# Three loads of an RWKV-6 and MLP kernel moved to other places in the sync queue, and one gate moved with them

## The chip, the cores and the metric

The kernel runs on one core of a Trainium2 chip. The metric is the device time of one execution in microseconds, as the median of several executions. The engines are named as the profile names them: PE multiplies matrices (PEld loads its weights), DVE and POOL do elementwise work, ACT does activations and copies, and SP here does nothing but issue DMA transfers.

## The reference

Two blocks run one after the other. The first is a recurrent attention with a per-channel decay, for 4 sequences of 768 tokens and 8 heads of 48 channels:

```python
for t in range(S):
    cur = np.einsum('bhd,bhe->bhde', u[None] * kt, vt)
    y[:, :, t] = np.einsum('bhd,bhde->bhe', rt, state + cur)
    state = wt[:, :, :, None] * state + np.einsum('bhd,bhe->bhde', kt, vt)
```

Its output, as 3072 tokens of 384 channels, goes through a two-layer network with 2048 hidden channels:

```python
h = x @ w_in
sp = np.maximum(h, 0.0) + np.log1p(np.exp(-np.abs(h)))
g = h * erf(sp)
return (g @ w_out).astype(np.float32)
```

## The kernel before

The work is cut into 12 steps. A step is 128 tokens of two of the four sequences, all heads. Step 0 is written out by `attend_first`, steps 1 to 4 by `attend`, the rest by `attend_late`. Inside a step the attention over 128 tokens is built in levels 1 to 6: at each level PE forms products of r and k (`level_products`, line 554), DVE multiplies r and k in place by products of decays (`scale`, line 330) and merges the new products into `own` (`take_level`, line 564, or two ACT copies, line 571, at level 6). POOL makes the products of decays (`tot_sb`, lines 352 and 404) out of the step's `w`. Then `own` is multiplied by `v` (line 586), the state is updated (line 660 on PE, lines 852 or 957 on DVE) and the output of the step is transposed into `xT`.

The network of step s runs beside the attention of step s+1. `hidden` makes its first product in eight pieces. Piece n multiplies `xT` with pair n of the weights `w_in` (line 1019, 12 matrix instructions in the trace), leaves the result in one of two PSUM buffers called `m`, and ACT copies it out to `h` (line 1028). With two buffers, piece n can start only when the copy of piece n-2 is done.

The weights arrive as 64-bit floats. They are loaded two rows of tiles at a time, called a pair here: eight pairs of `w_in` (0 to 7), then eight of `w_out` (8 to 15). `convert` turns a pair into 32-bit floats in five stages: **l**, the load of the pair as two transfers of 384 KB each into one of three `words` buffers (line 147, called from `load`); **b** and **r**, two ACT instructions on the loaded words (lines 257 and 265); **h**, a DVE shift (line 274); **o**, a POOL addition (line 287). **j** is h followed by o. The table `CONVERT` says which stages are sent at which level of a step. For step 1 (`CONVERT[1]`) each level from the second to the fifth sends "j" early, that is, right after `scale`, and "brl" at `place`, after `take_level`:

```python
(("j", "br"),) + (("j", "brl"),) * 4 + (("j", "l"), ("", ""), ("", ""), ("", "brl")),
```

So at level 2 of step 1 the early "j" belongs to pair 3 and the late "brl" means b and r of pair 4 and the load of pair 5; at level 3 the same for pairs 4, 5 and 6; at level 4 for pairs 5, 6 and 7. The b and r of a pair stand on ACT ahead of the copy (line 1028) of a piece: those of pair 5 ahead of the copy of piece 2, those of pair 6 ahead of that of piece 3.

Engines run their instructions in the order in which they are written (`manual_schedule`). All transfers spoken of here are issued by SP, one after the other, and an issue that waits holds back all issues behind it. A **gate** is a one-element copy by POOL (line 242 or 185) or ACT (line 240) into the buffer that a transfer will fill: the transfer then cannot be issued before the copy is done, and the copy waits for the value that it copies.

The order of the loads of interest in SP's queue before the change is: pair 2 (gate on `seen`, line 829), pair 3 (gate on `xT` by ACT, line 634), pair 4 (line 635), `v` of step 1 (line 186, behind the gate in `load_third`, line 185, which copies an element of the new state `S_next`), pair 5, the two halves of r and k of step 2 (line 924), `w` of step 2 (line 925), pair 6, pair 7, pair 8. The state's sum `S_next` is written by DVE at line 852, in `pending`, which `attend` calls at level 2 of step 1 (line 903), before the early "j" of that level (line 905).

`w` of step 2 is read first by POOL at line 404, `v` of step 1 by PE at line 586 of step 1, and r and k of step 2 by ACT at line 382.

Of the kernel before, what the change touches and what calls it, by code (L numbers as in the profile page):

```python
# [61 lines left out]
def kernel(  # L62
# [14 lines left out]
    nc = tc.nc  # L77
# [51 lines left out]
    turns = {"next": 0}  # L129
# [10 lines left out]
    loaded = {}  # L140
# [3 lines left out]
    def load_halves(dst, src):  # L144

        for i in range(2):
            nc.sync.dma_start(out=dst[:, i], in_=src[:, i])

    def load_w(s):
        ws[s] = ins.tile([P, JP, C], FP32, name="w")  # L150
        nc.sync.dma_start(out=ws[s][:], in_=rkw[s][:, 2])
# [25 lines left out]
        nc.scalar.copy(t[:, 0, 0, 0:1], behind)  # L177
        load_halves(t, rkw[1])

    def load_third(behind):  # L180

        t = ins.tile([P, 2, JP, C], FP32, name="in")
        vt = ins.tile([P, NH, D], FP32, name="v")
        loaded[2] = t, vt
        nc.gpsimd.tensor_copy(out=loaded[1][1][:, 0, 0:1], in_=behind)
        load_v(1)

    def load_v(s):

        vt = loaded[s][1]  # L190
        nc.sync.dma_start(out=vt[:], in_=v[s])
# [29 lines left out]
    def convert(weights):  # L221

        held = {}
        plain = weights[0][1].dtype == FP32
        signed = len(weights) // 2

        def load(i, behind=None, by_scalar=False):
            if i >= len(weights):  # L230
                return
            dst, src = weights[i]
            if plain:
                nc.sync.dma_start(out=dst, in_=src)
                return
            words = wide.tile([P, 2, DM, 2], I32, name="words", bufs=3)
            if behind is not None:
                to = words[:, 0, 0, 0:1].bitcast(FP32)
                if by_scalar:
                    nc.scalar.copy(to, behind)  # L240
                else:
                    nc.gpsimd.tensor_copy(out=to, in_=behind)
            load_halves(words[:].rearrange("p i n two -> p i (n two)"), src.bitcast(I32))
            held[i] = {"words": words}

        def scale_high(i, part=slice(0, 2)):


            if i not in held:
                return  # L250
            if i < 2:
                base = ps_m.tile([P, NP * C], FP32, name="m")[:, :DM]
            else:
                base = y[:].rearrange("p e q j t -> p e (q j t)")[:, :, :DM]
            high = held[i]["words"][:, part, :, 1].bitcast(FP32)
            if i < signed:
                nc.scalar.activation(base, high, AF.Prelu, scale=2.0**-112, alpha=-(2.0**32))
            else:
                nc.scalar.mul(out=base, in_=high, mul=2.0**-112)
            held[i].setdefault("bases", []).append((base.bitcast(I32), part))  # L260

        def scale_low(i):
            if i in held:
                rest = wide.tile([P, 2, DM], I32, name="rest", bufs=2)
                nc.scalar.mul(  # L265
                    out=rest[:], in_=held[i]["words"][:, :, :, 0].bitcast(U32), mul=2.0**-29
                )
                held[i]["rest"] = rest

        def shift(i):  # L270
            if i in held:
                base, part = held[i]["bases"].pop(0)
                into = weights[i][0].bitcast(I32)[:, part]
                nc.vector.tensor_scalar(
                    out=into if i < signed else base, in0=base, scalar1=3, scalar2=None,
                    op0=ALU.logical_shift_left,
                )
                if i >= signed:
                    nc.vector.scalar_tensor_tensor(
                        out=into, in0=held[i]["words"][:, part, :, 1], scalar=-(1 << 31),  # L280
                        in1=base, op0=ALU.bitwise_and, op1=ALU.bitwise_or,
                    )

        def add(i):
            if i in held:
                into = weights[i][0].bitcast(I32)
                nc.gpsimd.tensor_tensor(
                    out=into, in0=into, in1=held.pop(i)["rest"][:], op=ALU.add
                )

        def join(i):
            shift(i)
            add(i)

        stages = {"l": load, "b": scale_high, "r": scale_low, "h": shift, "o": add, "j": join}
        done = {"l": 5, "b": 2, "r": 2, "j": 2}

        def send(what):
            for stage in what:
                stages[stage](done[stage])  # L300
                done[stage] += 1

        return stages, send

    def rows(e, n=D):
        return slice(e * EP, e * EP + n)

    def at(e, p):

        return rows(e ^ p & 1)  # L310
# [215 lines left out]
    def parts_of(s):  # L526

        c, i = divmod(s, SPC)
        in_t, vt = loaded[s]
        made, tots, tot = ready[s]  # L530
        ends = tot.rearrange("p (n h) -> p n h", h=NC)
        return c, in_t, vt, made, states[i][c % 2], states[i][1 - c % 2], ends
# [5 lines left out]
    def first_pair(x, n):  # L538

        return turns["first"][:, n // NP, x, n % NP]  # L540
# [59 lines left out]
    def through_state(s, xT):  # L600

        c, in_t, _, _, S, _, _ = parts_of(s)
        for h, state in enumerate((S, middle)):
            if not (c or h):
                continue
            t = slice(h * HC, (h + 1) * HC)
            for j, q in ((0, 2), (1, 2), (1, 0), (0, 0)) if not s else np.ndindex(NJ, NP // 2):
                q = q if not s else 2 * q
                for e in range(NE):
                    for p in (q + e, q + 1 - e):  # L610
                        n = j * NP + p
                        nc.tensor.matmul(  # L612
                            y[at(e, p), e, p // 2, j, t],
                            lhsT=state[rows(e), n, :],
                            rhs=(in_t[:, 0, n] if s else first_pair(0, n))[rows(e), t],
                            start=False, stop=True, skip_group_check=True,
                        )

        y3 = att.tile([P, UNIT], FP32, name="y3", bufs=1)
        nc.scalar.copy(y3[:].rearrange("p (j t) -> p j t", j=NJ), y[:, 1, 1])  # L620
        parts = y[:, 0, 0], y[:, 0, 1], y[:, 1, 0]
        by_kk = [xT[:, kk, :].rearrange("p (j t) -> p j t", j=NJ) for kk in range(KT)]
        if not s:

            def hop():
                for kk in range(KT):
                    nc.tensor.matmul(
                        parts[kk], lhsT=apart[:, kk],
                        rhs=y3[:].rearrange("p (j t) -> p j t", j=NJ),
                        start=False, stop=True, skip_group_check=True,  # L630
                    )
                for kk in range(KT):
                    nc.scalar.copy(by_kk[kk], parts[kk])
                stages["l"](3, xT[:, KT - 1, 0:1], True)
                stages["l"](4)

            turns["hop"] = hop
            return
        for kk in range(KT):
            nc.scalar.copy(by_kk[kk], parts[kk])  # L640
        by_scalar = {(kk, 1) for kk in range(KT) if s <= DIRECT}
        for kk in range(KT):
            n = D // KT
            for e in range(NE):
                queue = nc.scalar if (kk, e) in by_scalar else nc.sync
                queue.dma_start(
                    out=xT[e * EP + D : (e + 1) * EP, kk, :],
                    in_=y3[e * EP + kk * n : e * EP + (kk + 1) * n, :],
                )
# [97 lines left out]
    def attend_first(xT):  # L747
# [5 lines left out]
        c, _, vt, made, S, S_next, ends = parts_of(0)  # L753
# [25 lines left out]
        behind = {3: (3,), 4: (4, 5), 5: (6,)}  # L779
# [47 lines left out]
        stages["b"](1, 1)  # L827
        fence()
        stages["l"](2, seen[:, 0:1])
        stages["h"](0)  # L830
        stages["h"](0)
        ps = [[products([P, NE, JP, HC], 1 - e)[:, e] for e in range(NE)]]
# [15 lines left out]
        def pending():  # L848
            part = products([P, NE, JP, HC], turns["next"])[:, 0]
            state_part(0, kT, ps + [[part] * NE], (1,))  # L850
            for e in range(NE):
                nc.vector.tensor_add(S_next[rows(e)], faded[1][rows(e)], part[rows(e), :, :D])
            load_third(S_next[:, 0, 0:1])

        turns["pending"] = pending

# [18 lines left out]
    def attend(s, xT, early, place, behind):  # L875

        c, in_t, vt, made, S, S_next, ends = parts_of(s)
# [9 lines left out]
        for level in range(near_log(s) + 1 if s == DIRECT else 1, LOG + 1):  # L887
# [34 lines left out]
            place(level - 1)  # L922
            if s == 1 and level == 2:
                load_halves(loaded[2][0], rkw[2])
                load_w(2)

        from_own(s, own, 1)
        ps = products([P, JP, P])
# [526 lines left out]
```

## Time and profile before

| | |
|---|---|
| median of 3 runs | 593.79 us (592.19 to 594.02) |
| the profiled execution, its own time | 592.98 us |
| its span, first to last instruction | 591.2 us |
| PE busy in the span | 581.1 us (98%) |
| DVE, ACT, POOL busy | 437.8, 361.1, 270.8 us |
| mean granted clock of PE | 0.997 |
| DMA traffic | 63.24 MB, mean 107 GB/s |

The profile's times count from the start of the span. A timeline row gives start, duration, engine, line, operation, output and input, and in brackets the engine's idle time before it with what ended it. A row of the chain of waits gives start, duration and what ran. A row of the stretches gives, for each engine, its busy time and number of instructions, then PE's granted clock, the busy share of the DMA engines and the GB/s that they moved. In the timeline of PE, the rows whose bracket names more than half a microsecond of waiting are, after the first 2 us, just one: piece 5 of the hidden product of step 0, at 50.91 us.

### The profile page before, as it was taken

The numbers are of one execution on the slowest core, as the hardware profiler recorded it, in microseconds if no ns is written. First come the engines' busy times: TensorE is split into PE (matmuls) and PEld (weight loads), VectorE is DVE, ScalarE is ACT, GpSimd is POOL, SyncE is SP. The second block draws the span as 40 slices with busy tenths as digits, with TensorE's granted clock in tenths as the row PEclk, the third lists the DMA queues.
The fourth block names the chain that finished last, engine by engine and source line by source line (L and its number), as shares of the span: only waits on it lengthen the run. The fifth ranks groups of instructions, "written<-read, shape, count | busy, mean of one in ns | idle before, by whom it ended". The sixth has DMA issues, their size and how long they took to land.

```text
span 591.2 us, 16634 instructions
## 1 busy us (share of the span) xinstructions
PE 581.1 (98%) x7256; PEld 499.3 (84%) x7256; DVE 437.8 (74%) x523; ACT 361.1 (61%) x474; POOL 270.8 (46%) x308
## 2 busy tenths in 40 slices
PE   8997999999999999999999999999999999999997
PEld 6686887678668758998998898898898898898997
DVE  6794795899996899799799799799799525023140
ACT  4656878635544598756766766766766764746710
POOL 4546372701498569559359359359359000000000
PEclk9998999999999999999999999999999999999999
DMA  7587462541423414334334334333331300000000
GB/s 243 177 286 284 160 220 74 202 144 19 143 76 133 114 58 154 62 122 155 73 119 158 73 119 158 73 120 122 73 119 43 73 15 20 3 19 15 1 27 28
DMA packets 54082, 63.24 MB, mean 107 GB/s; under 512 B 35161, under 2 KB 40569, under 8 KB 52985
## 3 DMA queue, kind: packets, MB, share of 16 engines
q1 hardware_dynamic: 53624, 61.98, 33.0%
q8 instruction: 57, 0.93, 0.6%
q10 hardware_dynamic: 384, 0.20, 0.1%
q14 instruction: 17, 0.13, 0.1%
HBM read 52.39 MB, written 8.69 MB: 103 GB/s over the span
## 4 chain that ended last, share of the span: by engine, by line
PE 84%; DVE 9%; DMA 3%; ACT 2%; issue 2%; POOL 0%; SPq 0%; DVEq 0%; POOLq 0%; ACTq 0%
PE m L1019 37%; PE m L1127 28%; PE m L1051 6%; PE pp L554 4%; PE y L586 2%; DVE in L330 2%; DMA words<-in_moe_w_in 2%; PE pp L660 2%; PE y L612 2%; PE m L861 1%; DVE words L469 1%; DMA rest<-in_w_rows 1%; DVE rk L465 1%; DVE sums L455 1%; ACT rest L265 1%
## 5 line engine op out<-in xcount | busy, mean ns | idle before, releaser
L1019 PE MATMUL m<-xT,w_in_sb 128*128 128x256 f32 x1152 | 258.3, 383 | 3.1 <-ACT h L1028 3.0
L1019 PEld LDWEIGHTS m<-xT,w_in_sb 128*128 128x128 f32 x1152 | 217.3, 191 | 34.2 <-issue 3.3
L1028 ACT COPY h<-m 128x512 f32<-128x512 f32 x96 | 55.5, 579 | 83.2 <-PE m L1019 83.2
L330 DVE TENSOR_TENSOR in<-in,tot_sb 128x1024 f32<-128x1024 f32 (+1 forms) x55 | 78.2, 1423 | 16.2 <-PE pp L554 13.9
L465 POOL TENSOR_TENSOR rk<-words 128x528 f32<-128x528 f32 (+3 forms) x28 | 42.4, 1516 | 91.2 <-DVE sums L455 80.8
L469 POOL TENSOR_TENSOR words<-words,rest 128x528 f32<-128x528 f32 (+10 forms) x77 | 78.2, 1015 | 6.0
L1051 PE MATMUL m<-w_out_sb,h 128*128 128x384 f32 x192 | 64.3, 491 | 0.0
L1051 PEld LDWEIGHTS m<-w_out_sb,h 128*128 128x128 f32 x192 | 35.7, 190 | 23.5
L1127 PE MATMUL m<-mixed,h 128*128 128x192 f32 x288 | 51.1, 331 | 0.0
L975 ACT ACT_TABLE_LOAD x36 | 46.2, 1283 | 2.9 <-issue 2.3
L1127 PE MATMUL m<-w_out_sb,h 128*128 128x192 f32 x272 | 47.5, 329 | 0.0
L1127 PEld LDWEIGHTS m<-mixed,h 128*128 128x128 f32 x288 | 46.6, 190 | 0.9
L979 ACT ACT_TABLE_LOAD x36 | 46.2, 1283 | 1.6 <-DVE room L1110 1.1
L1127 PEld LDWEIGHTS m<-w_out_sb,h 128*128 128x128 f32 x272 | 44.3, 190 | 0.4
L1127 PE MATMUL m<-w_out_sb,room 128*128 128x192 f32 x256 | 44.2, 326 | 0.0
L554 PEld LDWEIGHTS pp<-in 48*64 48x64 f32 (+1 forms) x2368 | 33.4, 126 | 12.0 <-issue 4.3
L1127 PEld LDWEIGHTS m<-w_out_sb,room 128*128 128x128 f32 x256 | 42.0, 190 | 0.0
L984 DVE TENSOR_TENSOR h<-h,y 128x1024 f32<-128x1024 f32 x17 | 20.7, 1215 | 28.3 <-ACT y L979 28.2
L975 ACT ACTIVATE room<-h 128x1024 f32<-128x1024 f32 x36 | 38.1, 1057 | 0.4
L404 POOL TENSOR_TENSOR tot_sb<-tot_sb 128x256 f32<-128x256 f32 (+4 forms) x50 | 36.1, 722 | 3.8
L984 DVE TENSOR_TENSOR h<-h,pp 128x1024 f32<-128x1024 f32 x19 | 23.1, 1213 | 19.6 <-ACT pp L979 19.6
L554 PE MATMUL pp<-in 48*64 48x32 f32 (+1 forms) x2368 | 37.1, 212 | 0.3 <-DVE in L330 0.2
(146 smaller groups left out, 823.4 us busy)
## 6 DMA issues: line engine op xcount, KB each, us to landing
in<-in_rkw SPq DMA_DIRECT2D x8, 1024.0 KB, 5.3
words<-in_moe_w_in SPq DMA_DIRECT2D x16, 384.0 KB, 7.3
words<-in_moe_w_out SPq DMA_DIRECT2D x16, 384.0 KB, 3.8
words<-in_rk_rows SPq DMA_DIRECT2D x8, 768.0 KB, 5.9
w<-in_rkw SPq DMA_DIRECT2D x11, 512.0 KB, 8.8
v<-in_v SPq DMA_DIRECT2D x12, 384.0 KB, 5.5
out<-o SPq DMA_DIRECT2D x23, 192.0 KB, 3.1
in<-in_rkw SPq DMA_DIRECT2D x7, 512.0 KB, 5.5
```

What stands on the lines that cost most here:

```text
L330: nc.vector.tensor_mul(halves, halves, view(tots[level - 1], 0, [[1, n], [2, nb], [0, half]]))
L404: nc.gpsimd.tensor_mul(new, pair[:, :, 0], pair[:, :, 1])
L465: engine.tensor_mul(terms[n], r[:, :, n:], k[:, :, : near - n])
L469: engine.tensor_mul(k[:, :, :m], k[:, :, :m], w[:, :, n : n + m])
L554: nc.tensor.matmul(to, lhsT=rk(1, n)[rows(e), s0 : s0 + m], rhs=right, start=True, stop=True,)
L975: nc.scalar.activation(sp_room, chunks[0], AF.Softplus)
L979: nc.scalar.activation(at, sp_room, AF.Erf)
L984: nc.vector.tensor_mul(h, h, at)
L1019: nc.tensor.matmul(ps[:, ff, :], lhsT=w_in_sb[:, g * FG + f + ff, kk * P : (kk + 1) * P], rhs=xT[:, kk, :], start=kk == 0, stop=kk == KT - 1,)
L1028: nc.scalar.copy(h[:, f : f + FT, :], ps[:])
L1051: nc.tensor.matmul(ps[j][:], lhsT=gs[g][:, f, j * C : (j + 1) * C], rhs=w_out_sb[:, g * FG + f, :], start=g + f == 0, stop=g == NG - 1 and ...
L1127: nc.tensor.matmul(to, lhsT=a[:, f], rhs=b[:, f], start=start and f == 0, stop=f == FG - 1, skip_group_check=True,)
```

## The change

`v` of step 1 is loaded right behind pair 2, with no gate. `w` of step 2 is loaded right behind pair 4, at the end of `hop`. The gate on the state's sum, which stood before the load of `v`, is kept as a value in `turns` and used by the next load of a pair that has no gate of its own, which is pair 5: the one-element copy now goes into pair 5's `words` buffer, at the place in POOL's stream where the load of pair 5 is written. The loads of `w` of step 3 and `v` of step 2 stay at level six of step 1, where they were.

```diff
-    def load_third(behind):
+    def load_third():
 
         t = ins.tile([P, 2, JP, C], FP32, name="in")
         vt = ins.tile([P, NH, D], FP32, name="v")
         loaded[2] = t, vt
-        nc.gpsimd.tensor_copy(out=loaded[1][1][:, 0, 0:1], in_=behind)
-        load_v(1)
...
             words = wide.tile([P, 2, DM, 2], I32, name="words", bufs=3)
+            if behind is None:
+                behind = turns.pop("gate", None)
             if behind is not None:
                 to = words[:, 0, 0, 0:1].bitcast(FP32)
...
                 stages["l"](3, xT[:, KT - 1, 0:1], True)
                 stages["l"](4)
+                load_w(2)
...
         fence()
         stages["l"](2, seen[:, 0:1])
+        load_v(1)
         stages["h"](0)
...
-            load_third(S_next[:, 0, 0:1])
+            load_third()
+            turns["gate"] = S_next[:, 0, 0:1]
...
             if s == 1 and level == 2:
                 load_halves(loaded[2][0], rkw[2])
-                load_w(2)
```

## The prediction

> **What bounds the kernel now.** I read the page's engine totals first: PE is busy for 581.1 of 591.2 us, so this change can only win what PE loses in the first 100 us, where the moved loads are. Then PE's idle times in the timeline. After the first 2 us there is a single long one, 2.99 us before piece 5 of step 0's hidden product (line 1019) at 50.91 us; the next longest that I found is 0.44 us, at 13.1. Third, the chain of waits through that place (start, duration, what ran):
>
> ```profile
> 38.45 0.27 SPq L147
> 38.71 0.04 issue
> 38.76 9.78 DMA words<-in_moe_w_in
> 48.56 0.04 ACTq L257
> 48.60 0.05 issue
> 48.64 0.85 ACT y L257
> 49.49 0.81 ACT rest L265
> 50.29 0.48 ACT h L1028
> 50.77 0.14 issue
> 50.91 4.39 PE m L1019 x12
> ```
>
> The reader is to see that PE waits for a PSUM buffer, that ACT frees it only after converting pair 6, and that pair 6 is a transfer issued at about 38.4 and landed at 48.56. From landing to PE it is 50.91 - 48.56 = 2.35 us. The last line also shows a second loss: other pieces of 12 instructions take 2.86 us in the timeline, this one 4.39, because the granted clock is 0.50 in the stretch from 50.67 to 54.08. So 2.99 + 1.53 = 4.5 us are at stake.
>
> Fourth, why pair 6 takes so long. SP's issues in the timeline:
>
> ```profile
> 35.49 0.33 SPq L191 DMA_DIRECT2D v<-in_v  x1
> 36.00 0.81 SPq L147 DMA_DIRECT2D words<-in_moe_w_in  x2
> 36.91 0.85 SPq L147 DMA_DIRECT2D in<-in_rkw  x2
> 37.80 0.43 SPq L151 DMA_DIRECT2D w<-in_rkw  x1
> 38.33 2.12 SPq L147 DMA_DIRECT2D words<-in_moe_w_in  x4
> ```
>
> Ahead of pair 6 stand v (384 KB), pair 5 (768), r and k of step 2 (1024) and w (512). The stretches of one microsecond (last two columns: DMA busy share and GB/s) say that the queue is empty before and full after:
>
> ```profile
> 35.00:36.00 1.00, 1.00 (x43) 0.67 (x44) 0.97 (x2) 0.02 (x1) 0.18 (x1) 1.00 0.00 0
> 36.00:37.00 1.00, 1.00 (x41) 0.92 (x35) 0.97 (x2) 0.76 (x1) 0.65 (x1) 1.00 0.62 71
> ...
> 40.00:41.00 1.00, 1.00 (x35) 0.91 (x28) 1.00 (x3) 0.00 (x0) 0.72 (x1) 1.00 0.69 184
> 41.00:42.00 1.00, 1.00 (x6) 0.87 (x5) 1.00 (x1) 0.45 (x1) 1.00 (x1) 1.00 1.02 410
> ```
>
> From 41 to 50 the rows stand between 386 and 418, mean 407 GB/s. So v and w, 896 KB or 0.92 MB, taken out of this queue are worth 0.92 / 0.407 = 2.25 us, if pair 5 starts when v did.
>
> **The change part by part.** It does not. The fifth view is POOL's timeline:
>
> ```profile
> 31.29 1.81 POOL L287 TENSOR_TENSOR w_in_sb<-w_in_sb,rest 128x768 int32<-128x768 int32 x1
> 35.28 0.18 POOL L185 COPY v<-s 128x1 f32<-128x1 f32 x1 [2.18 <-DVE s L852]
> 36.35 1.83 POOL L287 TENSOR_TENSOR w_in_sb<-w_in_sb,rest 128x768 int32<-128x768 int32 x1 [0.89 <-DVE w_in_sb L274]
> 40.28 1.81 POOL L287 TENSOR_TENSOR w_in_sb<-w_in_sb,rest 128x768 int32<-128x768 int32 x1 [2.10 <-DVE w_in_sb L274]
> ```
>
> Line 185 is the old gate, written in `pending`, ahead of level 2's early "j", whose addition (pair 3) is the row at 36.35. The new gate is written where pair 5's load is, in the late "brl" of that level, so it stands behind that addition. The copy then runs from 38.2 (36.35 + 1.83) and SP issues pair 5 at 38.3, where v was issued at 35.49 and pair 5 at 36.00. Behind the gate on POOL waits only the addition of pair 4, which DVE releases at 40.28 anyway; behind pair 5 on SP wait r and k, pairs 6 and 7.
>
> v behind pair 2: one issue (0.33 us, row at 35.49) after pair 2's two (22.12 to 22.93), and 0.39 MB / 0.407 = 1.0 us of transfer. The rows from 26 to 28 show 9 and 15 GB/s, and pair 3 is not issued before 28.01. Nothing: covered by that hole, and should the hole be gone, pair 3 lands up to 1.0 us later than now, against 1.5 us between ACT's wait for it (32.81) and DVE's shift of it (35.24), which waits for the state's sum. v is read at 55.23. w behind pair 4: its 512 KB take 1.3 us behind transfers which end at about 35.2 (rows 34 and 35: 77 and 0 GB/s), so it ends at 36.5, ahead of the new start of pair 5. Nothing as well; without that hole it would cost pair 5 its 1.3 us. Its reader, POOL line 404 at 46.65, waited 0.63 us for it and POOL is then idle again: nothing gained on the path.
>
> The start of pair 6. Before: v was issued at 35.49 and landed 3.0 us later, at 38.5; the 3072 KB behind it (pair 5, r and k, w, pair 6) were in at 48.56, after 10.05 us, of which 3.15 MB / 0.407 = 7.7 us is full rate and 2.3 us loss (the row at 40, and pieces of transfers behind it, pairs 7 and 8, that land before pair 6's last piece). After: pair 5 is issued at 38.3, its first half lands at 41.3 by the same 3.0 us, its second at 42.3; 2176 KB (2.23 MB) follow the first half. Lower end, no loss: 5.5 us, landing at 46.8. Upper end, the whole loss again: 7.8 us, 49.1. In proportion (10.05 x 2176 / 3072 = 7.1) it would be 48.4. The dip at 40 comes as the stream passes from weights to r and k, and that passage stays, so the loss does not shrink in full proportion: I take the middle of 48.4 and 49.1, 48.7. That is 0.15 us **later** than now, and piece 5 starts at 48.7 + 2.35 = 51.05. The 2.25 us of bytes are given back by 2.8 us of later start.
>
> Pair 5 lands at 42.3, and ACT's instruction on it, now at 41.55 after a wait of 3.11 us, moves by 0.8. ACT's block of work behind it ended at 45.53, so it is free for pair 6 at 46.3 even at the lower end. The copy of piece 2 (43.18 to 43.75) moves to 44.55, PE would wait 0.25 us before piece 4 (now 44.30); DVE's shift at 43.10 and the scale behind it move by 0.8, and PE's level 6 products (47.16 to 47.92) end at 48.7. All of this fills time that PE idles away now: nothing on the path.
>
> The clock. PE's gap becomes 51.05 - 48.7 = 2.3 us instead of 2.99, with some 0.7 us in pieces before it. If the clock stays up, piece 5 takes 2.86 for 4.39; the line 586 products may then start when ACT's copies of line 571 end (52.73 + 1.17 = 53.9), against 55.23: a gain of up to 1.5. The ends are 0 and -1.5. The rows that I have are a gap of 0.44 with no drop and one of 2.99 with a drop; 2.3 lies 0.73 of the way to the second, so I take 0.27 x 1.5 = 0.4 us of gain.
>
> The Trainium skill, "TensorE: Matmul & The Clock Gate" (The HAM clock gate), says that the array falls to half clock after a whole idle window of about 3.4 us, free-running. The drop here lasts 54.08 - 50.67 = 3.41 us, which agrees, but the window before it held 0.67 us of PE work, which by the page's wording should have kept the clock. By the page a gap of 2.3 us never drops it, and the sum would be +0.15 - 1.5 = -1.35, an estimate; by the trace it is unsettled.
>
> Sum: +0.15 - 0.4 = -0.25 us. What follows is data-dependent on this place (PE waits for nothing over half a microsecond later), so it passes to the end. The profiled execution took 592.98 us, 1.8 around its span, and lies 0.8 under the median, inside the runs' own spread of 1.8 us. Put on the median: 593.79 - 0.25 = 593.5.
>
> **The rivals.**
> Fast start, no drop: the loss disappears from the transfers and the clock stays up. For: the loss is no property of the bytes, and PE's work at 48 splits the gap. Against: the passage from weights to r and k stays. Price: 46.8 against 48.56 is -1.75, with -1.5: 590.5.
>
> The gate does what the words say: pair 5 hangs on the sum alone, issue at 35.5. Then pair 6 lands 2.8 us earlier than in my sum, the gap goes: -2.99 - 1.5 = -4.5, 589.3. Against it stands the order of the code, engines running in order.
>
> Slower, by one mechanism: pair 5 starts still later. The place is POOL's addition ahead of the gate, which also takes 2.68 us in this trace (same line on w_out, at 68.69), 0.85 more, and a load started onto an empty queue can take longer: the second half of pair 3 took 4.3 us, where I have 3.6 for pair 5's: 0.7 more. With the whole loss pair 6 lands at 49.1 + 0.85 + 0.7 = 50.65, 2.1 us later: 595.9. It decides from a landing after 50.3 on, 1.8 us later than now. For it: the queue does empty. Against: the addition at this place took 1.83.
>
> **How the numbers follow.** 0.3% of the time is 1.8 us, about what a measurement of this kernel can tell from no change. My forecast, within it: 0.50. Fast start with no drop: 0.30, and the gate on the sum alone: 0.06; these are the faster cases, 0.36. The slower rival: 0.14. The range reaches down to 590.5, which leaves out the gate's rival alone, and up to 595.3, which leaves out the last part of the slower one; the forecast's own is 592.1 (no drop, -1.65 with a landing at 48.4) to 594.3 (landing at 49.1, drop).
>
> **What would show it.** In the profile after: POOL's line 242 copy directly behind the addition at 36.35; pair 5 issued near 38.3; a hole with no DMA traffic from about 36.5 to 39; ACT's line 257 on pair 5 at about 42.4 and on pair 6 between 48.2 and 49.2; PE's gap before piece 5 at 2 to 2.5 us; POOL's line 404 no longer waiting for w. I am wrong if pair 5 is issued before 37, if pair 6 lands before 47.5 or after 50, or if PE finds a new wait later than 56 us.

## The result and the profile after

The changed kernel took 593.49 us (median of 12 runs, 592.60 to 595.89) beside 593.35 us of the kernel before on the same chip (12 runs): a ratio of 1.0002 with a 95% interval of 0.9983 to 1.0021. Measured once more later, it took 594.75 us (12 runs) beside 593.47 (29 runs), a ratio of 1.0018 (0.9999 to 1.0037). Both lie within 0.3%. The forecast, 593.5 us and no change, was right. Two of its terms were not, and that the first median meets it to 0.01 us is luck: the second lies 1.26 us higher. Of the loads only two change their place, `v` and `w`; pair 5 keeps its own and takes the gate.

The profiled execution of the changed kernel took 595.89 us, its span is 594.1. Part of that does not come from the change: PE's timeline (start, duration, work, and in brackets the idle time with what ended it) has a wait 2 us before the first moved issue.

```profile
21.91 0.66 PE L586 MATMUL y<-own,v 64*48 64x64 f32 x32 [1.02 <-DMA v<-in_v]
```

This is `v` of step 0, which landed late. The state's sum therefore ends at 36.42 us here (DVE line 854, the first of DVE's rows below, 35.31 + 1.11) and at 35.21 before, in DVE's timeline there:

```profile
34.10 1.11 DVE L852 TENSOR_TENSOR s<-faded,pp 48x384 f32<-48x384 f32 x2
```

The same late `v` shows in the second profile of the changed kernel (a wait of 1.32 us) and in one of a kernel that holds nothing of the change (0.86 us, the one before with half of piece 4 computed twice, below). From here on times of different kernels are compared **from the end of that sum**.

SP's issues of the changed kernel in the timeline:

```profile
23.94 0.43 SPq L189 DMA_DIRECT2D v<-in_v  x1
29.12 1.75 SPq L147 DMA_DIRECT2D words<-in_moe_w_in  x4
30.97 0.62 SPq L151 DMA_DIRECT2D w<-in_rkw  x1
40.55 0.81 SPq L147 DMA_DIRECT2D words<-in_moe_w_in  x2
41.47 0.84 SPq L147 DMA_DIRECT2D in<-in_rkw  x2
42.40 1.89 SPq L147 DMA_DIRECT2D words<-in_moe_w_in  x4
```

`v` and `w` are where the change puts them. Pair 5 is the row at 40.55, which is 4.1 us after the sum; before, it was issued 0.8 us after it. POOL's timeline says what it waited for, and DVE's says what the copy waited for:

```profile
37.56 1.84 POOL L287 TENSOR_TENSOR w_in_sb<-w_in_sb,rest 128x768 int32<-128x768 int32 x1 [3.26 <-DVE w_in_sb L274]
39.34 1.19 POOL L242 COPY words<-s 128x1 f32<-128x1 f32 x1
41.49 1.81 POOL L287 TENSOR_TENSOR w_in_sb<-w_in_sb,rest 128x768 int32<-128x768 int32 x1 [0.97 <-DVE w_in_sb L274]
48.82 2.02 POOL L404 TENSOR_TENSOR tot_sb<-w 128x512 f32<-128x512 f32 x1
```

```profile
35.31 1.11 DVE L854 TENSOR_TENSOR s<-faded,pp 48x384 f32<-48x384 f32 x2
38.68 1.80 DVE L330 TENSOR_TENSOR in<-in,tot_sb 128x1024 f32<-128x1024 f32 x1
```

The gate stands directly behind the addition of pair 3, as its place in the code says. But this one-element copy takes 1.19 us, where the old gate took 0.18. It ends at 40.53, and DVE's scale ends at 40.48 (38.68 + 1.80). POOL's line 404 has no bracket: it no longer waits for `w`.

The stretches of one microsecond (last two columns: DMA busy share and GB/s) show the empty queue. The two longer rows, which the section on why speaks of, show the clock (the column before them) in piece 5:

```profile
38.00:39.00 1.00, 1.00 (x42) 0.93 (x35) 1.00 (x2) 1.00 (x2) 1.00 (x1) 1.00 0.01 4
39.00:40.00 1.00, 1.00 (x6) 0.87 (x5) 1.00 (x1) 0.81 (x2) 1.00 (x2) 1.00 0.00 0
40.00:41.00 1.00, 1.00 (x7) 0.84 (x5) 1.00 (x2) 0.00 (x0) 0.52 (x1) 1.00 0.00 0
...
50.35:53.76 3.41, 1.17 (x61) 1.03 (x48) 1.58 (x3) 2.94 (x5) 2.06 (x3) 1.00 0.83 275
53.76:57.18 3.42, 3.42 (x10) 2.72 (x9) 2.31 (x2) 2.30 (x4) 3.19 (x6) 0.50 0.81 288
```

Last, ACT's and PE's timelines, the end of the chain that the prediction followed:

```profile
45.03 0.87 ACT L257 ACTIVATE y<-words 128x768 f32<-128x768 f32 x1 [5.22 <-DMA words<-in_moe_w_in]
46.62 0.56 ACT L1030 COPY h<-m 128x512 f32<-128x512 f32 x1
...
50.81 0.85 ACT L257 ACTIVATE y<-words 128x768 f32<-128x768 f32 x1 [1.43 <-DMA words<-in_moe_w_in]
```

```profile
47.34 2.83 PE L1021 MATMUL m<-xT,w_in_sb 128*128 128x256 f32 x12 [1.07 <-ACT h L1030]
50.09 0.76 PE L554 MATMUL pp<-in 48*32 48x32 f32 x64
53.10 4.51 PE L1021 MATMUL m<-xT,w_in_sb 128*128 128x256 f32 x12 [2.25 <-ACT h L1030]
```

ACT waits for pair 5 until 45.03 and for pair 6 until 50.81. PE's single wait of 2.99 us has become two, 1.07 us before piece 4 and 2.25 us before piece 5, and piece 5 still runs its first part at half clock (4.51 us). From the sum:

| us after the end of the state's sum | before | after | after, second profile |
|---|---|---|---|
| pair 5 issued | 0.8 | 4.1 | 4.1 |
| ACT on pair 6 | 13.4 | 14.4 | 14.2 |
| piece 5 on PE | 15.7 | 16.7 | 16.4 |
| from pair 5's issue to ACT on pair 6 | 12.6 | 10.3 | 10.0 |

The last row is what the change was worth: 2.3 us and more. The first is what it cost: 3.3 us.

### The profile page after: what moved, and what is told of

The parts are those of the page before. It is cut to its first block, busy times and chain, and to the rows that moved or that the text cites. A ratio compares the mean times of both kernels' runs of the same rounds, so it can differ in the third digit from the quotient of the medians.

```text
span 594.1 us, 16635 instructions
## 1 busy us (share of the span) xinstructions
PE 581.4 (98%) x7256; PEld 499.1 (84%) x7256; DVE 436.7 (73%) x523; ACT 360.8 (61%) x474; POOL 272.8 (46%) x308
## 4 chain that ended last, share of the span: by engine, by line
PE 60%; ACT 3%; issue 1%; DVE 1%; ACTq 0%; DVEq 0%
PE m L1129 28%; PE m L1021 27%; PE pp L554 2%; PE y L586 1%; PE y L612 1%; PE pp L661 1%; ACT room L977 1%; ACT L981 1%; ACT L977 1%; PE pp L1129 0%; ACTq L647 0%; ACT pp L981 0%; DVE in L330 0%; ACT y L981 0%; PE pp L674 0%
```

## The experiments

Each ratio is against the kernel before on the same chip. One profile belongs to each kernel. Line numbers shift by a few with the edits.

### The gate ahead of the addition

The load of pair 5, gate and all, is written where the old gate stood, in `pending`.

```diff
-            if i >= len(weights):
+            if i >= len(weights) or i in held:
                 return
...
-            if behind is None:
-                behind = turns.pop("gate", None)
...
             load_third()
-            turns["gate"] = S_next[:, 0, 0:1]
+            stages["l"](5, S_next[:, 0, 0:1])
```

The first lines keep pair 5 from being loaded a second time at its old place.

> All of the change is kept, but pair 5's load, with its gate on the state's sum, is written where the sum is, so that the gate stands on POOL ahead of the addition of pair 3 and not behind it. Theory (the late start of pair 5 gives back what the removed bytes save): SP issues pair 5 within 0.4 us of the end of the state's sum, some 3 to 4 us earlier than in the changed kernel counted from that sum; pair 6 lands 3 to 4 us earlier counted from it; PE's gap before piece 5 falls from 2.2 to under 0.7 us and the clock stays up; the time falls by 2.5 to 4.5 us, to 589 to 591. Rival (the gap does not set the end, later work does): the gap goes, the time stays within 1 us of before. Rival (the landing hangs on the last DMA engine's arrears and not on the start): pair 6 lands less than 1.5 us earlier.

Measured: 590.13 us (11 runs) beside 593.50 (28 runs), ratio 0.9956 (0.9933 to 0.9979), where 589 to 591 was expected. The timeline:

```profile
34.78 1.11 DVE L852 TENSOR_TENSOR s<-faded,pp 48x384 f32<-48x384 f32 x2
...
35.95 0.18 POOL L240 COPY words<-s 128x1 f32<-128x1 f32 x1 [2.18 <-DVE s L852]
...
36.16 1.37 SPq L147 DMA_DIRECT2D words<-in_moe_w_in  x2
...
47.54 0.89 ACT L255 ACTIVATE y<-words 128x768 f32<-128x768 f32 x1 [1.43 <-DMA words<-in_moe_w_in]
...
49.86 2.83 PE L1019 MATMUL m<-xT,w_in_sb 128*128 128x256 f32 x12 [1.28 <-ACT h L1028]
```

The sum ended at 35.89. The copy takes 0.18 us again, pair 5 is issued 0.3 us after the sum, and ACT is on pair 6 11.7 us after it, 2.7 us earlier than in the changed kernel where 3 to 4 were expected. A gap of 1.28 us stays before piece 5; under 0.7 was expected. The place of the gate is the cause of the late start; its effect on the landing was overestimated.

### No gate at all

```diff
-            if behind is None:
-                behind = turns.pop("gate", None)
...
-            turns["gate"] = S_next[:, 0, 0:1]
```

> The changed kernel without any gate on pair 5; its load waits only for its buffer and for SP's order. Theory: pair 5 is issued at about 32, right behind w of step 2, or when ACT is done with pair 2's words; pair 6 lands before 45; no gap of PE over 0.7 us between 30 and 60; time 2.5 to 4.5 us under before, within 0.7 us of the kernel with the gate ahead of the addition, since there is no gap left to win. Rival (the gate protects something: loads that come earlier delay pairs 3 and 4 or the second step's r and k): PE's wait moves to an earlier piece and the time is 1 us or more above that kernel.

Measured: 589.79 us (6 runs), ratio 0.9935 (0.9916 to 0.9953).

```profile
34.51 1.11 DVE L852 TENSOR_TENSOR s<-faded,pp 48x384 f32<-48x384 f32 x2
...
32.23 1.09 SPq L147 DMA_DIRECT2D words<-in_moe_w_in  x2
...
35.55 3.66 SPq L147 DMA_DIRECT2D words<-in_moe_w_in  x4
...
45.98 0.88 ACT L255 ACTIVATE y<-words 128x768 f32<-128x768 f32 x1 [1.44 <-DMA words<-in_moe_w_in]
...
48.30 2.83 PE L1018 MATMUL m<-xT,w_in_sb 128*128 128x256 f32 x12
```

Pair 5 is issued 3.4 us **ahead** of the end of the sum (35.62), right behind the loads before it. ACT is on pair 6 at 45.98; a time under 45 was expected. Piece 5 waits for nothing and takes 2.83 us: no loss is left here. With a start 7.5 us earlier than in the changed kernel, counted from the sum (4.1 after it against 3.4 ahead of it), pair 6 is on ACT only 4.0 us earlier (14.4 less 10.4). The queue no longer empties (327 to 422 GB/s in each microsecond from 33 to 46), and pair 6 is held by something else: it goes into the buffer that pair 3 had, ACT's last instruction on pair 3 ends at 35.52, and SP issues pair 6 at 35.55.

### The kernel before without its gate

This one has none of the moved loads. One line is taken out of the kernel before.

```diff
-        nc.gpsimd.tensor_copy(out=loaded[1][1][:, 0, 0:1], in_=behind)
         load_v(1)
```

> The kernel before with nothing moved but without the gate on the load of v, so that v follows pair 4 and pair 5 follows v with no wait for the state's sum. Theory (the start of pair 5 decides, the bytes ahead of pair 6 count for 2.25 us): pair 5 is issued 3 to 4 us earlier than before, PE's gap falls under 1 us, 590 to 591. If the moves of v and w add nothing once the gate is gone, it equals the changed kernel without a gate (589.8) within 0.5 us; if their bytes still count, it is 0.7 to 2 us above it. Rival (the gate is what keeps r and k of step 2 and pair 5 from delaying pairs 3 and 4): slower than before.

Measured: 589.35 us (6 runs) beside 593.58 (18 runs), ratio 0.9935 (0.9913 to 0.9956).

```profile
31.32 1.18 SPq L147 DMA_DIRECT2D words<-in_moe_w_in  x2
...
46.27 0.88 ACT L256 ACTIVATE y<-words 128x768 f32<-128x768 f32 x1 [2.29 <-DMA words<-in_moe_w_in]
...
48.60 2.83 PE L1018 MATMUL m<-xT,w_in_sb 128*128 128x256 f32 x12 [0.85 <-POOL tot_sb L403]
```

Its median is within 0.5 us of the version with both loads moved and no gate. So once the queue is not held, moving `v` and `w` adds nothing that can be measured, and nearly all of the 4.5 us that were at stake here was lost to the gate: 4.2 come back by this one line. Here too pair 6 is issued when its buffer comes free (ACT is done with pair 3 at 35.12, SP's issue is at 35.15), 0.1 us after the sum, which ended at 35.06; with `v` and `w` moved it is 0.1 us ahead of it. These two, with the gate gone, are the best versions found, 0.65% faster than the kernel before.

### `v` and the gate moved, `w` left

```diff
                 stages["l"](4)
-                load_w(2)
...
                 load_halves(loaded[2][0], rkw[2])
+                load_w(2)
```

> v behind pair 2 and the gate on pair 5 as in the change, w of step 2 back ahead of pair 6. Theory: pair 5 starts as late as in the changed kernel and 512 KB more stand ahead of pair 6, so pair 6 lands 1.3 us later than there (0.52 MB at 0.407 MB per us) counted from pair 5's issue, and the time is 1.0 to 2.0 us above before. Rival (bytes ahead of pair 6 do not matter, one slow DMA engine does): same time as the changed kernel within 0.5 us.

Measured: 595.23 us (12 runs), ratio 1.0035 (1.0015 to 1.0055). In its profile pair 5 is issued 4.1 us after the sum, as in the changed kernel, and ACT is on pair 6 15.6 us after it, 1.2 us later; 1.3 was expected for the 512 KB of `w`. PE waits 3.00 us before piece 4 and 2.25 before piece 5. This part of the change alone is slower than no change: the start is 3.3 us later and only `v`'s 384 KB are out of the way, worth 1.0 us by the prediction's rate; 2.3 us later is the sum, 2.2 (15.6 less 13.4) were measured.

### `w` alone moved

The other half: the kernel before with `load_w(2)` at the end of `hop`; `v` and its gate stay.

```diff
                 stages["l"](4)
+                load_w(2)
...
                 load_halves(loaded[2][0], rkw[2])
-                load_w(2)
```

> w of step 2 behind pair 4, everything else as before: v with its gate on the state's sum, pair 5 right behind v. Theory: the start stays and 512 KB go, so pair 6 lands 1.3 us earlier than before counted from the state's sum, PE's gap falls from 3.0 to about 1.7 us, and the time falls by 1.3 us if the clock still drops, by up to 2.8 if it does not: 590.5 to 592. Rival: within 0.5 us of before.

Measured: 591.85 us (12 runs), ratio 0.9970 (0.9948 to 0.9992). The time is better, but its profile doesn't bear out the size: ACT is on pair 6 13.2 us after the sum, 0.3 earlier than before, where 1.3 was expected, and the gap is split into 1.49 us before piece 4 and 1.34 before piece 5. The two issues of pair 5 took 1.65 us in that execution, instead of 0.81, so one profile may understate it. By the medians this part alone is faster than the whole change, though their intervals (up to 0.9992 here, from 0.9983 there) still overlap. Part of the gain can be the clock: by the mean clock of the runs, 6 of the 12 had a drop, against 21 of the 28 of the kernel before that ran beside them. How its transfers gain stays open.

### The gate on ACT, at the same place

Is the 1.19 us a matter of the value that is copied, or of POOL? The copy goes to ACT, same value, same buffer.

```diff
             if behind is None:
                 behind = turns.pop("gate", None)
+                by_scalar = behind is not None
```

> The changed kernel with the gate's one-element copy made by ACT instead of POOL, at the same place of the program, where it stands behind the r of pair 4. Theory (POOL's addition and then DVE's scale hold the gate back): the copy takes 0.2 us on ACT, SP issues pair 5 about 1.0 us earlier counted from the end of the state's sum (3.1 us after it, not 4.1), pair 6 lands 1 us earlier, and the time falls by 0.8 to 2.0 us against the changed kernel. Rival (SP or the queue, not the gate, sets the issue): issue and time unchanged within 0.4 us.

Measured: 593.02 us (12 runs) beside 593.58 (18 runs), ratio 0.9982 (0.9965 to 0.9999).

```profile
34.83 1.11 DVE L855 TENSOR_TENSOR s<-faded,pp 48x384 f32<-48x384 f32 x2
...
38.76 0.17 ACT L241 COPY words<-s 128x1 f32<-128x1 f32 x1
38.96 0.80 SPq L147 DMA_DIRECT2D words<-in_moe_w_in  x2
...
51.44 4.39 PE L1022 MATMUL m<-xT,w_in_sb 128*128 128x256 f32 x12 [2.10 <-ACT h L1031]
```

The sum ended at 35.94. On ACT the copy takes 0.17 us and pair 5 is issued 3.0 us after the sum (3.1 expected), 1.1 earlier than from POOL; ACT is on pair 6 13.2 us after the sum, 1.2 earlier, and piece 5 starts 15.5 us after it. So the copy's long duration was worth about its 1.1 us of start, though the interval of the time overlaps that of the changed kernel. The other 2.7 us (3.0 less the 0.3 of the gate ahead of the addition) are the place: on ACT the copy stands behind the "br" of pair 4.

### The changed kernel once more

No edit; a second set of runs and a second profile.

> The changed kernel again, nothing altered: its profile was of an execution in which the load of the first v came late (PE waited 1.02 us for it at 20.9, before anything that the change touches). Theory (addition, then DVE's scale, hold the gate): the gate's copy ends within 0.1 us of the end of the scale that DVE runs at that time, SP issues pair 5 4.0 to 4.2 us after the end of the state's sum, PE waits 0.8 to 1.3 us before piece 4 and 1.8 to 2.6 us before piece 5. Median within 0.3% of before. Rival (the late copy was that execution's own): pair 5 is issued 3.0 to 3.3 us after the sum.

Measured: the 594.75 us above. POOL's and DVE's timelines in this execution:

```profile
39.76 1.18 POOL L242 COPY words<-s 128x1 f32<-128x1 f32 x1
...
39.05 1.85 DVE L330 TENSOR_TENSOR in<-in,tot_sb 128x1024 f32<-128x1024 f32 x1
```

The copy ends at 40.94 and the scale at 40.90. Everything lies 0.4 us later than in the first profile, and the copy still ends with the scale.

### The gap filled with PE work

Does piece 5's half clock come from PE's idle time? Two kernels compute the products of level 6 of step 1 three times instead of once, ahead of the gap: one made from the kernel before, one from the changed kernel, with the same edit. The repetition is extra work and changes no value.

```diff
             if s == 1 and level == LOG:
+                for _ in range(2):
+                    level_products(pp, rk, level)
                 early(level - 1)
```

> The kernel before, with the level 6 products of step 1 formed three times over (the same values written again), so that about 1.5 us of PE's gap before piece 5 is filled with work and nothing else is moved. Theory (the drop of the clock after the gap costs up to 1.5 us in the executions in which the gap falls well into one 3.41 us interval of the clock's grid): piece 5 starts when it did, the clock stays at 1.00 in every profile, its 12 instructions take 2.83 to 2.86 us, and the median falls by 0.7 to 1.5 us, to 592.0 to 592.8. Rival (ACT's copies behind it hide the slow piece): within 0.4 us of before.

> The changed kernel with the same filling. Theory: clock at 1.00, median 0.5 to 1.5 us under the changed kernel, and 0.7 to 1.3 us above the filled kernel before, since with the clock out of the account only the later landing of pair 6 is left (about 1 us by the two profiles). Rival (the change itself is worth nothing either way, whatever the clock): the two filled kernels agree within 0.4 us. In the profile the gate's copy again lasts about 1.19 us and ends with DVE's scale.

Both missed: 596.45 us (7 runs), ratio 1.0058 (1.0038 to 1.0078), from the kernel before, and 597.24 us (6 runs), ratio 1.0061 (1.0038 to 1.0084), from the changed one. In the first one PE's timeline says why:

```profile
48.10 1.41 PE L554 MATMUL pp<-in 48*32 48x32 f32 x143
53.44 0.90 PE L554 MATMUL pp<-in 48*32 48x32 f32 x49 [3.93 <-issue]
```

PE stops for 3.93 us in the middle of the repeated products, and the profile shows no engine and no data that it waits for. In that stretch the trace has a 16 KB packet on the instruction queue (q8 in the page's list of queues), at 51.03 us, with the weights' transfers at 412 to 418 GB/s ahead of it; PE goes on 1.3 us after it has ended (51.03 + 1.07 = 52.10). That PE waited for its own instructions is an inference from this. Here the filler made a longer wait than it was to fill. The profile of the second kernel is another case:

```profile
46.86 5.46 PE L1023 MATMUL m<-xT,w_in_sb 128*128 128x256 f32 x12 [2.73 <-ACT h L1032]
52.25 1.53 PE L554 MATMUL pp<-in 48*32 48x32 f32 x143
54.08 0.63 PE L554 MATMUL pp<-in 48*32 48x32 f32 x49 [0.30 <-issue]
```

There PE's long wait lies before piece 4, ahead of the filler, which therefore fills nothing; the clock is at 0.50 from 45.77 to 52.59, and piece 4 takes 5.46 us. The stop in the repeated products is 0.30 us only, and PE goes on 1.4 us after the end of a packet on the same queue (51.72 + 0.97 = 52.69), after 1.3 in the first kernel. The question of the clock was left to the next two kernels.

### The gap filled with fewer, longer matrix instructions

Half of piece 4 is computed twice (6 more instructions, 1.29 us more), again once from each kernel and with the same edit.

```diff
-                for ff in range(FT):
+                for ff in (0, 0, 1) if cut and g == 1 and not f else range(FT):
```

> The kernel before, with the first half of piece 4 of step 0's hidden product computed twice (the same values written again): 6 matrix instructions in the trace, 1.4 us of PE work, hardly any instructions to fetch. It delays PE's level 6 products into the gap and moves nothing else. Theory (a drop of the clock costs 1.5 us; 16 of 18 executions of before that came with a clock had one): the gap before piece 5 falls to about 1.5 us, the clock stays at 1.00, piece 5 takes 2.86 us, and the median falls by 0.8 to 1.5 us. Rival (the slow piece is hidden): within 0.4 us of before.

> The changed kernel with the same half piece computed twice. Theory: no drop of the clock in most executions; the median falls by 0.3 to 1.0 us against the changed kernel (8 of 12 of its executions had a drop), and with the clock out of the account this kernel is 0.5 to 1.3 us above the filled kernel before, the price of the later landing of pair 6 alone. Rival: the two filled kernels agree within 0.3 us.

From the kernel before: 592.49 us (12 runs), ratio 0.9986 (0.9964 to 1.0007); the median is 1.0 us lower, as expected, but the interval holds 1. In its profile the gap is 1.33 us, piece 5 takes 2.83 us and the clock stays up; by the mean clock of the runs, it dropped in 3 of 12, against 60 of the 75 runs of the kernel before. From the changed kernel: 594.83 us (12 runs), ratio 1.0028 (1.0011 to 1.0044), level with the changed kernel's 594.75, where 0.3 to 1.0 us less was expected. In its profile too the clock stays up, with gaps of 0.83 and 1.06 us; but it dropped in 10 of its 12 runs, where few were expected. With more PE work ahead of piece 5 the drop became rare in the first kernel. In the second it did not; its filler runs after the wait for piece 4 and makes up nothing of that one, but why the drop stays is not explained.

## Why the prediction was right, and where not

**Where the gate stands: right.** The prediction put the copy behind the addition of pair 3, not at the sum, from the order of the code. The profile after shows it there, and the kernel with the gate ahead of the addition shows what it is worth: 0.46% or 2.7 us between the two ratios (0.9956 against 1.0002).

**Bytes given back by the late start: right.** From pair 5's issue to ACT on pair 6 the prediction had 10.4 us (38.3 to 48.7), measured were 10.3 and 10.0. The hole without traffic is there, the gap before piece 5 is 2.25 and 2.29 us for 2.3, and the moved loads themselves cost nothing: the version with both moved and no gate equals the one with neither moved and no gate. The margin that the prediction gave pair 3 shrank, though: ACT takes it up 0.9 and 1.4 us ahead of the end of the sum in the two profiles after, 2.4 ahead of it before. On the prediction's own scale (before's time, the sum ending at 35.21) ACT is on pair 6 at 49.6 and 49.4, above the 48.2 to 49.2 that it named and under the 50 from which on it was to be wrong. Read off the profiles as they stand, 50.81 and 51.01, it would have been past 50; 1.2 and 1.6 us of that had come about ahead of the sum.

**The issue of pair 5: mis-sized by 1.0 us.** The step "the copy then runs from 38.2 and SP issues pair 5 at 38.3" took the copy at next to nothing. It takes 1.18 to 1.19 us in each of the profiles that have it at this place, and in each it ends within 0.05 us of the end of DVE's scale. From the sum: 1.14 us to the addition, 1.84 of addition, 1.13 more of the copy, 4.1 in all, not 3.1. That POOL's copy can't finish beside DVE's scale is read from this coincidence, from the copy's 0.18 us where no scale runs (35.95, with DVE in a shift) and from ACT's 0.17; the scale itself was not taken away. The opposite direction fits. The scale takes 1.22 us with POOL idle (the changed kernel at 248.08 us), 1.80 where 0.72 us of an addition lie in it (39.40 less 38.68), and 2.52 where 1.43 do (before: 40.66, addition to 42.09): about 1.2 plus most of the overlap. And the addition of 2.68 us at 68.69, which the prediction's slower rival was priced by, begins inside a scale too (68.47 to 69.69), as does its twin in the changed kernel at 107.10 (2.67 us for 1.83, scale from 106.88 to 108.10).

The Trainium skill, "Advanced Engine Details and Errata" (Miscellaneous Facts, GPSIMD Details), says that POOL shares a read and a write interface with DVE and conflicts with DVE instructions that have two inputs in SBUF. The scale is one, and the rows agree; the page gives no time for it.

The row that could have priced it was in the trace of before. In the timeline there, an early gate lies beside DVE's scale of step 0:

```profile
13.50 0.50 POOL L242 COPY words<-own 128x1 f32<-128x1 f32 x1 [0.71 <-DVE own L564]
...
13.25 1.30 DVE L323 TENSOR_TENSOR in<-in,tot_sb 128x512 f32<-128x512 f32 x2
```

The same one-element copy takes 0.50 us here and ends at 14.00, about when the first of the two scale instructions does (13.25 + 0.65 = 13.90).

**Piece 4's wait: mis-sized.** 0.25 us was forecast; it is 1.07 and 0.86, from the same late issue. Piece 5 starts 1.0 and 0.7 us later than before, counted from the sum, not 0.15.

**The clock: the gain of 0.4 did not come.** One interval at half clock costs 1.53 us, as in the trace (4.39 less 2.86): by their mean clock, the runs of the kernel before without a drop average 591.74 us (15 runs), those with one 593.27 (37 runs); the other 23 had more than one and average 595.0. The changed kernel had a drop in 8 of its first 12 runs and in all of the second 12, 20 of 24, the kernel before in 60 of 75. So 0.27 x 1.5 is to be replaced by nothing. By these traces it is not the gap's length that decides but how much PE work is left in each interval of a grid of 3.41 us. The grid is read from the drops: in both profiles of the changed kernel the clock drops once in piece 5 (53.76 and 54.57) and once after the last instruction (593.07 and 593.87), 539.3 us later each time, which is 158 intervals of 3.413. In the profile of the kernel with `v` alone the only drop is after the last instruction, at 591.83:

```profile
591.00:591.83 0.83, 0.00 (x0) 0.00 (x0) 0.00 (x0) 0.00 (x0) 0.00 (x0) 1.00 0.00 0
591.83:592.50 0.67, 0.00 (x0) 0.00 (x0) 0.00 (x0) 0.00 (x0) 0.00 (x0) 0.50 0.00 0
```

539.3 us before it is 52.53, so its intervals begin at 42.29, 45.70 and 49.12. These stretches are the interval ahead of the drop and the one of the drop in the kernel before, and then the same of the kernel with `v` alone, which has a gap of 3.00 us (44.44 to 47.44, in two intervals) and no drop (first number after the length: PE busy; third from the end: clock):

```profile
47.25:50.67 3.42, 0.67 (x64) 0.55 (x64) 1.15 (x2) 2.03 (x4) 1.41 (x3) 1.00 0.94 369
50.67:54.08 3.41, 3.17 (x8) 2.57 (x9) 2.76 (x3) 3.21 (x6) 3.29 (x3) 0.50 0.79 250
```

```profile
42.29:45.70 3.41, 2.15 (x69) 1.59 (x67) 0.96 (x1) 0.53 (x1) 0.00 (x0) 1.00 1.01 383
45.70:49.12 3.42, 1.68 (x8) 1.53 (x9) 3.07 (x3) 3.37 (x8) 1.97 (x2) 1.00 1.02 396
```

With 0.67 us of PE work in an interval (before) and with 1.17 (after, shown above) the clock drops for the next one; with 1.68 and 2.15 it doesn't. The other profiles put the border near half an interval but not at one number: 1.28 (the second profile) and 1.56 (the gate on ACT) are followed by a drop, and so is 1.78 in the changed kernel with the repeated products:

```profile
42.35:45.77 3.42, 1.78 (x68) 1.26 (x66) 0.89 (x2) 1.18 (x2) 0.00 (x0) 1.00 1.02 383
45.77:49.18 3.41, 2.32 (x6) 1.90 (x7) 3.41 (x3) 2.79 (x8) 2.61 (x2) 0.50 1.04 402
```

Of these 1.78 us, 1.14 are the 64 small products of line 554, where the 1.68 are all of the long ones of line 1021; whether that is the reason was not tested. The rule of the Trainium skill, "TensorE: Matmul & The Clock Gate" (The HAM clock gate), which the prediction weighed and left unsettled, is not what these runs show: by it only an idle window drops the clock, and here windows with a fifth to a half of PE work do.

**The sum.** By its own terms with what they measured, +0.7 to +1.0 us for piece 5 and 0 for the clock; the medians say +0.14 and +1.28 us against the kernel before. Runs with the same number of drops say much the same: the changed kernel's four without one average 593.04 us, 1.3 above those of the kernel before, its 12 with one 594.06, 0.8 above, though these come from several chips. All of this is within the 1.8 us taken as no change, so the forecast held, with a term wrong by 1.0 us and another by 0.4, both to the same side: the range carried it, not the sum. Of the rivals, "fast start, no drop" fell with the copy's 1.19 us, "the gate on the sum alone" was not what the changed kernel does; it is the kernel with the gate ahead (590.13 us, forecast 589.3), and "pair 5 starts still later" came true in its direction, but through the copy instead of the addition, and too little to decide: ACT on pair 6 is 1.0 us later from the sum, and it named 1.8 as the point.

Open are why the drop stays in the changed kernel when half of piece 4 is computed twice, and how much of the difference between its two medians is chance.

## What to carry to other kernels

A gate costs what its place in its engine's stream costs: list what stands ahead of it, and what another engine runs beside it, before asking what it waits for. Taking bytes out of a queue pays only if the queue's start stays where it was, and here removing the gate, one line, was worth more than moving any load. When a moved instruction is priced, look for the same instruction in other company in the trace, not for its shortest row.

## What the hardware showed unexpectedly

- A one-element copy on POOL took 1.19 us instead of 0.18 beside a DVE multiplication with two inputs, and ended with it.
- The clock drops on a grid of 3.41 us after an interval that is not idle: 1.17 us of PE work in it did not hold the clock, 1.68 did, but 1.78, most of it small matrix instructions, did not.
- In the one profile of the kernel before with 128 more small matrix instructions, PE stopped for 3.93 us with no engine or data to wait for; it stopped in a microsecond in which the DMA engines moved 412 GB/s. In the changed kernel the same 128 show a stop of 0.30 us, and 6 longer instructions (1.29 us of work against 1.52) show none in either.
